# One weight load of a decode kernel, split by partitions into loads of 112, 8 and 8 rows

## The chip, the cores and the metric

The kernel runs on one core of a Trainium2 chip. Its time is device microseconds; the median of three runs before the change is 128.26 us (128.17 to 128.54). The profile is of one further execution of the same program, which took 128.43 us.

## The reference

One token (x, 576 numbers) is normalized and goes through two branches, whose results are added to it.

```python
xn = _layernorm(x)                                   # x: (1, 1, 576)
q  = (xn @ wq)                                       # 32 heads of 128
k, v = the last 4096 of 65536 cached positions       # 16 heads, each used by two query heads
A  = softmax(q k^T * 128**-0.5) v, flattened, @ wo   # wo: (4096, 576)
z  = gelu(xn @ w_in)                                 # w_in: (576, 4608)
B  = (z[:2304] * (w_sp * layernorm(z[2304:]) + b_sp)) @ w_out
out = x + A + B
```

All tensors are bfloat16. The kernel has to read 16.8 MB of keys, 16.8 MB of values and about 17.4 MB of weights, and it writes 576 numbers.

## The kernel before

**Loads.** All large loads are issued from the SP queue, in the order in which they are written at lines 106 to 124: w_q in three pieces, the first block of keys (k0) in two pieces, k1, v0, k2, v1, k3, w_in in two pieces, v2, v3, w_o in three, w_out in five. A block of keys or values holds four heads, 4 MB, 32 KB for each of the 128 partitions. Three tiny loads (the row x_row and two single numbers, ws2) go through the ACT queue at lines 77 to 80.

**The load that is changed.** w_q is read as 1152 half rows of 2048 numbers; partition p holds half rows 9p to 9p+8, which lie one after the other in memory. `load` at line 91 cuts this by half rows:

```python
load(wq_t, wq_v, 2048, (0, 2, 4, NR))      # line 106, NR = 9
```

This makes three loads over all 128 partitions: two of two half rows (8 KB for a partition) and one of five (20 KB for a partition, 2560 KB in all).

**Buffers.** Large tiles share two pools, `small` and `large`, of two buffers each. So k2 can only be issued when the transposes of k0 have ended, v1 when the products of w_q have ended, and so on down the list; SP waits at such a load, and everything after it in the list waits with it. Each load takes the next of eight completion semaphores in turn; a load that takes one again waits until the load that had it last has landed.

**Work on the loads.** `q_ps` (line 223) multiplies the nine half rows by the normalized x, four matmuls for each. `turn(b)` (line 214) transposes a block of keys in eight VectorE instructions; `scores(b)` (line 259) multiplies them by q and prepares the softmax; `values(b)` (line 293) multiplies by the values. The order is written out by hand: turn 0, scores 0, turn 1, scores 1, values 0, and so on to scores 3, then the gated branch (`z_all`, line 317, and `gate`), values 2 and 3, the products with w_o and the first eight rows of w_out (line 391), and last the other ten rows of w_out (line 399), the copy `res` (line 408) and the store of the result (line 409).

## Time and profile before

| What | Value |
|---|---|
| Median of three runs | 128.26 us |
| Profiled execution | 128.43 us, its span 126.6 us |
| Read from memory | 50.96 MB |
| DMA, mean over the span | 403 GB/s |
| PE (matmuls) busy | 76.3 us, 60% |
| DVE (VectorE) busy | 65.6 us, 52% |
| ACT busy | 10.2 us, 8% |
| Mean granted TensorE clock | 0.794 |

The span runs from the first to the last instruction; 1.8 us of the execution's time lie outside of it. Engines in the profile: PE is the matmul, PEld the load of its weights, DVE is VectorE, ACT ScalarE, SP the engine that issues the loads, and SPq its queue. The trace also has a record for every packet that a DMA engine moved (start, duration, bytes, queue) and for every step of a completion semaphore; it does not say which of the 16 DMA engines a record belongs to.

### The profile page before, as it was taken

How to read it: one execution, taken by the hardware profiler on the slowest of the kernel's cores; microseconds unless marked ns; L12 is line 12 of the kernel's file. 1: busy time of each engine (PE TensorE's matmuls, PEld its weight loads, DVE VectorE, ACT ScalarE, POOL GpSimd, SP SyncE). 2: the span in 40 equal slices, each digit the busy share in tenths (PEclk: the TensorE clock that was granted, in tenths of full speed). 3: DMA queues.
4: the chain of work that ended last, by engine and by line, in shares of the span. 5: the costliest groups of instructions: out<-in, count | busy, mean ns of one | idle time of the engine just before them, and what ended most of it. 6: DMA issues, size and time to landing. Idle time of an engine off the chain costs nothing.

```text
span 126.6 us, 1380 instructions
## 1 busy us (share of the span) xinstructions
PE 76.3 (60%) x562; PEld 35.0 (28%) x562; DVE 65.6 (52%) x133; ACT 10.2 (8%) x19; POOL 3.9 (3%) x10
## 2 busy tenths in 40 slices
PE   3241435995179946339963729991960865757470
PEld 3120211331023413313422403330730432423240
DVE  6660069996599844079953169944438400040010
ACT  4010000000300003100003100003000110100010
POOL 8400000000000000000000000000000000000000
PEclk9999999999756999955999975698555595865555
DMA  4999999998998999989999899898999989999930
GB/s 101 427 445 440 430 424 450 430 497 383 448 471 352 476 404 435 476 362 476 404 435 476 382 459 454 384 454 387 487 393 440 455 366 418 433 405 423 400 138 0
DMA packets 3187, 51.03 MB, mean 403 GB/s; under 512 B 365, under 2 KB 622, under 8 KB 1134
## 3 DMA queue, kind: packets, MB, share of 16 engines
q1 hardware_dynamic: 3176, 50.96, 94.8%
q8 instruction: 4, 0.07, 0.2%
q14 instruction: 1, 0.01, 0.0%
q10 hardware_dynamic: 6, 0.00, 0.0%
HBM read 50.96 MB, written 0.00 MB: 402 GB/s over the span
## 4 chain that ended last, share of the span: by engine, by line
DMA 78%; PE 10%; DVE 6%; SPq 2%; ACT 1%; issue 1%; ACTq 0%
DMA k<-in_A_k_cache_dram 37%; DMA v<-in_A_v_cache_dram 27%; DMA wout<-in_B_w_out_dram 14%; PE s L259 8%; DVE kt L214 5%; PE pv L293 1%; ACT p L279 1%; SPq L93 1%; SPq L99 1%; DVE sm L262 1%; PE tr L270 0%; PE su L283 0%; PE fin L399 0%; DVE res L408 0%; DVE m L272 0%
## 5 line engine op out<-in xcount | busy, mean ns | idle before, releaser
L259 PE MATMUL s<-kt,zq 128*128 128x512 bf16 x128 | 38.4, 465 | 10.3 <-DVE kt L214 10.1
L214 DVE STREAM_TRANSPOSE kt<-k 128x1024 f32<-128x1024 f32 x32 | 36.6, 1208 | 3.1 <-DMA k<-in_A_k_cache_dram 3.1
L259 PEld LDWEIGHTS <-zq 128*128 128x128 bf16 x128 | 14.6, 114 | 32.9 <-issue 23.0
L293 PE MATMUL pv<-v,pt 128*32 128x512 bf16 x128 | 10.2, 477 | 1.9 <-DMA v<-in_A_v_cache_dram 1.9
L279 ACT ACTIVATE p<-sm,nm 128x1024 bf16<-128x1024 f32 x4 | 4.6, 1147 | 71.1 <-DVE nm L275 71.1
L304 DVE TENSOR_TENSOR o_t<-op,rm 128x8 bf16<-128x8 f32 x4 | 0.7, 166 | 15.0 <-PE op L301 15.0
L223 PE MATMUL q_ps<-wq,xw 128*32 128x512 bf16 x36 | 4.2, 627 | 6.6 <-DMA wq<-in_A_wq_dram 4.3
L262 DVE CUSTOM_DVE_ANT_1 sm<-s,cm 128x512 f32<-128x512 f32 x8 | 5.4, 672 | 4.7 <-PE s L259 4.7
L281 DVE STREAM_TRANSPOSE pt<-p 128x1024 bf16<-128x1024 bf16 x4 | 5.0, 1245 | 5.4 <-ACT p L279 5.4
L283 PE MATMUL su<-sel,l 128*128 128x8 f32 x8 | 1.8, 293 | 7.6 <-ACT p L279 7.6
L301 PE MATMUL op<-selu,pvs 128*128 128x8 f32 x32 | 4.2, 259 | 2.8 <-ACT pvs L298 2.8
L293 PEld LDWEIGHTS <-pt 128*32 128x32 bf16 x128 | 3.7, 118 | 6.6 <-issue 3.2
L301 PEld LDWEIGHTS op<-selu,pvs 128*128 128x128 f32 x32 | 3.9, 191 | 4.8 <-ACT pvs L298 4.8
L391 PE MATMUL acc<-wo,o_p 128*1 128x288 bf16 x64 | 4.4, 439 | 0.8 <-DMA wo<-in_A_wo_dram 0.8
L395 DVE COPY acc_sb<-acc 128x288 f32<-128x288 f32 x1 | 0.5, 459 | 8.4 <-PE acc L391 8.4
L227 DVE CAST q_sb<-q_ps 128x512 bf16<-128x512 f32 x1 | 0.7, 692 | 7.5 <-PE q_ps L223 7.5
L317 PE MATMUL z<-win,xw 128*32 128x288 bf16 x72 | 4.5, 446 | 0.0
L270 PE MATMUL tr<-ident_f,m 128*128 128x128 f32 x8 | 1.9, 326 | 3.9 <-DVE m L268 3.9
L223 PEld LDWEIGHTS <-xw 128*32 128x32 bf16 x36 | 1.4, 130 | 8.6 <-issue 8.6
L283 PEld LDWEIGHTS su<-sel,l 128*128 128x128 f32 x8 | 1.4, 218 | 8.4 <-ACT p L279 8.4
L298 ACT COPY pvs<-pv 128x512 f32<-128x512 f32 x4 | 2.3, 586 | 13.0 <-PE pv L293 13.0
L346 PE MATMUL sz_ps<-sz,ones_f 128*128 128x2 f32 x2 | 0.6, 362 | 4.6 <-DVE sz L343 4.6
(95 smaller groups left out, 45.1 us busy)
## 6 DMA issues: line engine op xcount, KB each, us to landing
v<-in_A_v_cache_dram SPq DMA_DIRECT2D x4, 4096.0 KB, 32.3
k<-in_A_k_cache_dram SPq DMA_DIRECT2D x3, 4096.0 KB, 30.6
win<-in_B_w_in_dram SPq DMA_DIRECT2D x1, 4608.0 KB, 34.2
k<-in_A_k_cache_dram SPq DMA_DIRECT2D x2, 2048.0 KB, 19.1
wo<-in_A_wo_dram SPq DMA_DIRECT2D x2, 2016.0 KB
wq<-in_A_wq_dram SPq DMA_DIRECT2D x1, 2560.0 KB, 12.6
wq<-in_A_wq_dram SPq DMA_DIRECT2D x2, 1024.0 KB, 6.9
wout<-in_B_w_out_dram SPq DMA_DIRECT2D x1, 1152.0 KB, 25.3
```

What stands on the lines that cost most here:

```text
L214: nc.vector.transpose(t[:].rearrange("p c n e -> p (c n e)").bitcast(FP32), kn[b][:, UK * DH * k:UK * DH * (k + 1)].bitcast(FP32).rearrang ...
L223: nc.tensor.matmul(q_ps[32 * g:32 * g + 32, :], lhsT=xw[:, r, :], rhs=wq_t[:, 2048 * r + 512 * g:2048 * r + 512 * (g + 1)], start=r == 0, ...
L259: nc.tensor.matmul(s_ps[:], lhsT=zq[:, b, ce, ZPAD - 8 * k4:ZPAD - 8 * k4 + P], rhs=kt[b, 4 * kk + k4][:, c, :, e], start=k4 == 0 and ce = ...
L262: nc.vector.tensor_tensor_reduce(out=sm[:, kk, :].rearrange("p (n s) -> p n s", s=HB), in0=s_ps[:].rearrange("p (n s) -> p n s", s=HB), in ...
L279: nc.scalar.activation(p[:], sm[:].rearrange("p k n -> p (k n)"), ACT.Exp, bias=nm[:], accum_out=l[:])
L281: nc.vector.transpose(p_t[b][:].rearrange("p k u m -> p (k u m)"), p[:])
L283: nc.tensor.matmul(su[:], lhsT=l[:].to_broadcast([P, P]), rhs=sel8[:], start=True, stop=True)
L293: nc.tensor.matmul(pv[32 * g:32 * g + 32, :].rearrange("p (n d) -> p n d", n=4), lhsT=p_t[b][:, kk, u, :], rhs=v4[:, kk, u, :, :], start=k ...
L298: nc.scalar.copy(pvs[:], pv[:])
L301: nc.tensor.matmul(op[:], lhsT=pvs[:, DH * u:DH * (u + 1)], rhs=selu[:, 8 * u:8 * u + 8], start=u == 0, stop=u == 3)
L317: nc.tensor.matmul(zp[i][32 * g:32 * g + 32, :], lhsT=xw[:, r, :], rhs=rhs, start=r == 0, stop=r == NR - 1, tile_position=(0, 32 * g))
L391: nc.tensor.matmul(acc[i][32 * g:32 * g + 1, :], lhsT=col, rhs=w[:, HW * i:HW * (i + 1)], start=n == 0 and g > 0, stop=n + 4 >= len(rows), ...
```

## The change

The last piece of w_q, five half rows for each partition, is no longer loaded for all 128 partitions at once, but in three loads: partitions 0 to 111, 112 to 119 and 120 to 127. Each moves the same 20 KB for a partition as before. The bytes, the tile, and all other instructions are the same; SP issues two loads more, at the third place of its list, and each later load takes the completion semaphore two further on in the round of eight.

```diff
     wq_t = unit("wq", LARGE)
-    load(wq_t, wq_v, 2048, (0, 2, 4, NR))
+    load(wq_t, wq_v, 2048, (0, 2, 4))
+    for a, e in ((0, 112), (112, 120), (120, P)):
+        nc.sync.dma_start(wq_t[a:e, 4 * 2048:], wq_v[a:e, 4 * 2048:])
     kn[0] = load_kv(A_k_cache, "k", 0, SMALL, (0, NU // 2, NU))
```

## The prediction

> **What bounds the kernel now.** I read the DMA row of the page first, then the chain of waits, then stretches, then single packets and landings.

> ```profile
> DMA  4999999998998999989999899898999989999930
> GB/s 101 427 445 440 430 424 450 430 497 383 448 471 352 476 404 435 476 362 476 404 435 476 382 459 454 384 454 387 487 393 440 455 366 418 433 405 423 400 138 0
> ```

> Each digit is 3.2 us. The DMA engines are full from the second slice to the last but one. The chain that ended last is 78% DMA, and its end shows what the kernel waits for:

> ```profile
> 71.19 34.61 DMA v<-in_A_v_cache_dram
> 105.80 0.02 issue
> 105.82 17.43 DMA wout<-in_B_w_out_dram
> 123.25 0.04 issue
> 123.29 0.32 PE fin L399 x4
> 123.61 0.02 issue
> 123.63 0.31 DVE res L408
> ```

> The last piece of w_out lands at 123.25, and 3.4 us (four matmuls, a copy, the store) follow to the span's end at 126.6. The stretches say the same with a number: a DMA share of 0.99 to 1.02 everywhere between 2 and 120 us.

> ```profile
> 2.00:14.00 12.00, 3.84 (x28) 2.46 (x29) 5.32 (x21) 1.58 (x3) 2.54 (x3) 1.00 0.99 412
> 14.00:24.00 10.00, 6.30 (x36) 2.48 (x36) 6.65 (x11) 0.00 (x0) 0.00 (x0) 1.00 1.02 439
> 71.00:106.00 35.00, 21.78 (x166) 11.03 (x166) 17.84 (x39) 3.15 (x7) 0.00 (x0) 0.69 0.99 424
> 106.00:120.00 14.00, 9.60 (x115) 4.29 (x111) 1.34 (x6) 0.59 (x1) 0.00 (x0) 0.62 1.00 418
> ```

> The packet records make it sharper. On one engine a packet starts 3 to 4 ns before its predecessor ends, so the records fall into 16 chains, one for each engine, and none has a hole from 1.8 us until its last packet. A 20 KB packet (one row of the changed load) takes 761 ns, 26.9 GB/s; 32 KB takes 1218 ns. At the end, when eleven engines are done, the other five go on at the same 51 ns for 1152 bytes: no engine gets faster when others stop. So the kernel's time is the work of its **slowest engine**, plus 3.4 us.

> Which engine is slowest? The 16 landings of the last load are eleven at 121.30 to 121.78, then 122.41, 122.92, 123.04, 123.17 and 123.25. Five engines are late, and what makes them late is fetched instructions:

> ```profile
> q8 instruction: 4, 0.07, 0.2%
> q14 instruction: 1, 0.01, 0.0%
> ```

> The four packets of q8 (16 KB, at 36.8, 73.2, 96.4 and 119.0 us) and the one of q14 (8 KB, 34.1 us) fall on five chains. Around the one at 36.8, the fetch takes 1099 ns and the next 32 KB packet 1681 instead of 1218: 1.5 us that this engine never makes up. At the landings of the last block of values the four engines hit by then stand 0.65 to 1.5 us behind the rest.

> **The change part by part.** Bytes are the same; what changes is who carries them, and where they go.

> *Rows for each engine.* A load over 128 partitions shows eight packets a chain. Small loads use fewer engines: both single numbers of ws2 lie on one chain, and the store of four rows has four packets and four landing steps. So 112 rows should be seven for each of 16 engines, and each load of eight rows one for each of the same eight, which I call A; B are the others. A then carries 9 rows instead of 8, B 7. At 761 ns a row that is +0.76 for A and -0.76 for B, plus some 10 ns for A's two more completion packets. [...]

> *Where the rows go.* This is the unknown that decides. In all loads of before, each engine has eight partitions to itself; 26.9 GB/s may be what an engine can carry or what the way into its partitions lets through, and the trace cannot tell these apart. In the new small loads eight engines write into eight neighbouring partitions at once. If the engine is the limit, a row takes 0.76 us there too. If eight partitions share one way, eight rows go one after another: 8 x 0.761 = 6.09 us for each small load. Nearest in the trace is that no group of eight partitions is ever filled at more than 26.9 GB/s, which speaks for the dear side; but neighbours may be spread over more ways than one. I take four rows to a way, 3.04 us a load, between the ends and on the dear side. A's share is then 7 + 4 + 4 = 15 row times instead of 8: 7 x 0.761 = +5.33 us.

> [...]

> *SP's list.* Two loads more, 0.43 us each by the third w_q load, move k0's first half from 2.09 to about 3.0. The new round of semaphores makes k0's second half wait for a tiny load (landed 5.36), k1 for the next (6.09) and v0 for the first piece of w_q (5.66). The engines have work queued until 18.6 us at that time, so this costs nothing; without that cover it would be up to 3 us. Every later load still waits for the load eight places ahead of it, which is the same one as before.

> *What waits for w_q.* Its last piece lands at 14.21 now, by the sum near 19.5. The rest of `q_ps`, the first transposes (19.12) and the issue of k2 (28.67) and v1 (29.36) slide by as much, and so do later issues that hang on transposes or products. The queue covers it: k2 would be issued at 34, and the engines have v0 to carry until 42.9; w_in moves from 50.8 to 56, with v1 queued until 62; the last piece of w_out from 105.8 to 111, with work queued until about 119. So no engine runs dry, and the delay of the slowest engine reaches the end once, not twice. PE and DVE are busy 60% and 52% and slide along.

> *The sum.* [...] Then 123.17 + 5.33 = 128.50 instead of 123.25, +5.25 us. The profiled execution would take 128.43 + 5.25 = 133.7; it lies 0.17 over the median, so **133.5 us**.

> **The rivals.**

> *1. The forecast: the eight engines share the way into eight partitions.* Two rows to a way instead of four and no late engine in A: 7 + 2 + 2 = 11 row times, +2.28, from 121.78 to 124.06, a gain of 0.8 at the end: 129.1. Four rows to a way, and B's next load in the way as well as clashes within the 112 rows: two or three row times more, about 135.5. Eight rows to a way would give 23 row times, +11.4 us, near 139.6; I leave that end out, as it has the whole of eight rows meet. Chance 0.55.

> *2. Each engine is its own limit, and late engines lie in A and B.* Then the 123.17 engine ends at 123.17 + 0.77 = 123.94: +0.7, **129.0 us**. For it: no row shows two engines slowing one another. Chance 0.19.

> *3. Each engine is its own limit, and all five late engines lie in B: faster.* B's last lands at 123.25 - 0.76 = 122.49, A's at 121.78 + 0.77 = 122.55, so -0.7: **127.6 us**. The split would be a balance: it gives the rows to engines that have about 1.5 us to spare. [...] It decides where no engine that lands after 122.48 is in A (123.25 - 0.77). Chance 0.18.

> *4. No change.* Engine-limited, and only the engine of 122.41 is in A: 122.41 + 0.77 = 123.18 against 123.25, **128.2 us**. That the split does not move rows at all (112 rows over 16 engines in some other way) comes out here too. Chance 0.08.

> **How the numbers follow.** About 0.3% (0.4 us) is what a measurement of this kernel can tell from no change. Faster is rival 3, 0.18; same is rival 4, 0.08; slower is the forecast and rival 2, 0.74. The range leaves rival 3 out: from 128.0 to 135.6. The forecast's own range is 129.1 to 135.6.

> **What the next profile would show.** Eight chains with nine packets of 20 KB, eight with seven. In the forecast: packets of 20 KB that take about 3 us instead of 0.76, w_q's last landing near 19.5 instead of 14.2, and from there all landings in two groups some 5 us apart. In rivals 2 to 4: all packets at 0.76, the last landing of w_q near 15.0, two groups 1.5 us apart. I would be wrong in the basis if an engine ran dry behind a late issue, or if the last landing moved otherwise than the slowest chain.

## The result and the profile after

The kernel became slower: 138.03 us (median of four runs, 137.28 to 138.26) against 128.23 us, a ratio of 1.0743 with a 95% interval of 1.0725 to 1.076, or +9.8 us. I had forecast +5.25 us, and a range that ended at 135.6.

The profiled execution took 138.26 us with a span of 136.4. The DMA rows of its page, 3.4 us a digit or number:

```profile
DMA  4999997999999999999999999999999999999920
GB/s 132 428 343 276 195 110 149 427 423 504 403 413 425 447 442 452 403 394 461 442 452 403 394 488 415 432 394 428 461 452 427 403 398 426 430 401 428 372 85 0
```

The engines are as busy as before, but from the third to the seventh slice (7 to 24 us) they move 110 to 343 GB/s instead of some 430. The digits do not show this loss, the bytes do: an engine whose packet takes several times as long still counts as busy (in the second stretch of the changed kernel below, a share of 1.03 at 122 GB/s). From 24 us on, both rows are as before. The same in two stretches, the first two lines from the kernel before, the others from the changed one (columns: stretch, length, the busy times of PE, PEld, DVE, ACT and POOL, clock, DMA share, GB/s):

```profile
7.20:15.80 8.60, 3.45 (x32) 1.43 (x36) 1.87 (x9) 0.00 (x0) 0.00 (x0) 1.00 1.02 437
15.80:23.00 7.20, 3.75 (x20) 1.36 (x13) 5.91 (x11) 0.00 (x0) 0.00 (x0) 1.00 1.01 435
```

```profile
7.20:15.80 8.60, 1.90 (x16) 0.67 (x16) 1.86 (x9) 0.00 (x0) 0.00 (x0) 1.00 1.01 267
15.80:23.00 7.20, 0.00 (x0) 0.00 (x0) 0.00 (x0) 0.00 (x0) 0.00 (x0) 1.00 1.03 122
31.00:120.00 89.00, 62.48 (x370) 28.06 (x369) 53.03 (x93) 8.03 (x15) 0.00 (x0) 0.77 1.00 430
```

The chain of waits of the changed kernel begins and ends so:

```profile
2.83 21.31 DMA wq<-in_A_wq_dram
24.14 0.14 issue
24.27 2.35 PE q_ps L225 x19
...
115.57 17.41 DMA wout<-in_B_w_out_dram
133.02 0.32 PE fin L401 x4
133.36 0.31 DVE res L410
```

The last piece of w_q lands at 24.14 instead of 14.21, 9.9 us later; the last piece of w_out at 132.98 (115.57 + 17.41) instead of 123.25, 9.7 us later. The whole loss arises before 24 us, and reaches the end once.

By packets: in the load of 112 rows each engine moves its seven rows of 20 KB in seven rounds, whose medians are 1.00, 1.31, 1.40, 1.27, 1.01, 1.18 and 1.37 us instead of 0.761 each. The 16 packets of the two loads of eight rows take 2.0 to 3.28 us, median 3.22: in the first load seven take 2.0 to 2.6, in the second all take 3.2 to 3.3, and the engine that ends last has 3.25 and 3.22. With the medians of the seven rounds, 8.53 us together, that makes 8.53 + 2 x 3.22 = 15.0 us, where eight rows took 6.1: +8.9. The last of these packets ends 9.2 us later than before; another 0.7 us lies between its end and its landing (1.08 us, before 0.38).

### The profile page after: what moved, and what is told of

It is laid out like the page before. It is cut to its first block, busy times and chain, and to the rows that moved or that the text cites. A ratio compares the mean times of both kernels' runs of the same rounds, so it can differ in the third digit from the quotient of the medians.

```text
span 136.4 us, 1383 instructions
## 1 busy us (share of the span) xinstructions
PE 78.0 (57%) x562; PEld 36.4 (27%) x562; DVE 65.3 (48%) x133; ACT 10.2 (7%) x19; POOL 3.9 (3%) x10
## 4 chain that ended last, share of the span: by engine, by line
DMA 53%; PE 31%; DVE 8%; ACT 3%; SPq 1%; issue 1%; ACTq 0%
DMA v<-in_A_v_cache_dram 24%; PE s L261 21%; DMA wq<-in_A_wq_dram 16%; DMA wout<-in_B_w_out_dram 13%; PE pv L295 4%; ACT p L281 3%; DVE kt L216 3%; PE q_ps L225 2%; DVE sm L264 2%; PE op L303 1%; PE tr L272 1%; DVE pt L283 1%; SPq L108 1%; PE su L285 1%; DVE m L274 1%
## 5 line engine op out<-in xcount | busy, mean ns | idle before, releaser
L261 PE MATMUL s<-kt,zq 128*128 128x512 bf16 x128 | 37.7, 464 | 7.1 <-DVE kt L216 7.1
L295 PE MATMUL pv<-v,pt 128*32 128x512 bf16 x128 | 12.7, 568 | 2.7 <-DMA v<-in_A_v_cache_dram 2.7
L303 PE MATMUL op<-selu,pvs 128*128 128x8 f32 x32 | 5.9, 311 | 2.8 <-ACT pvs L300 2.8
L303 PEld LDWEIGHTS op<-selu,pvs 128*128 128x128 f32 x32 | 5.5, 259 | 6.0 <-ACT pvs L300 6.0
L393 PE MATMUL acc<-wo,o_p 128*1 128x288 bf16 x64 | 3.7, 387 | 0.4 <-DMA wo<-in_A_wo_dram 0.4
L319 PE MATMUL z<-win,xw 128*32 128x288 bf16 x72 | 3.7, 381 | 0.0
```

What stands on the lines that cost most here:

```text
L261: nc.tensor.matmul(s_ps[:], lhsT=zq[:, b, ce, ZPAD - 8 * k4:ZPAD - 8 * k4 + P], rhs=kt[b, 4 * kk + k4][:, c, :, e], start=k4 == 0 and ce = ...
L295: nc.tensor.matmul(pv[32 * g:32 * g + 32, :].rearrange("p (n d) -> p n d", n=4), lhsT=p_t[b][:, kk, u, :], rhs=v4[:, kk, u, :, :], start=k ...
L303: nc.tensor.matmul(op[:], lhsT=pvs[:, DH * u:DH * (u + 1)], rhs=selu[:, 8 * u:8 * u + 8], start=u == 0, stop=u == 3)
L319: nc.tensor.matmul(zp[i][32 * g:32 * g + 32, :], lhsT=xw[:, r, :], rhs=rhs, start=r == 0, stop=r == NR - 1, tile_position=(0, 32 * g))
L393: nc.tensor.matmul(acc[i][32 * g:32 * g + 1, :], lhsT=col, rhs=w[:, HW * i:HW * (i + 1)], start=n == 0 and g > 0, stop=n + 4 >= len(rows), ...
```

## Experiments

Each diff shows the lines that stand at the place of `load(wq_t, wq_v, 2048, (0, 2, 4, NR))`; all else is the kernel before. Theory P: several engines that write into neighbouring partitions at once share a way of about one engine's rate (26.9 GB/s: 20 KB in 0.761 us before). Its rivals: S, the loads more in SP's list; E, nine rows against seven; R, the reading; later N, odd row counts. Row times are medians of 20 KB packets, with one row of before at 0.761 us.

**The same cut by columns (e1).**

```diff
+    load(wq_t, wq_v, 2048, (0, 2, 4))
+    for a, e in ((0, 8960), (8960, 9600), (9600, 10240)):
+        nc.sync.dma_start(wq_t[:, 8192 + a:8192 + e], wq_v[:, 8192 + a:8192 + e])
```

> The last piece of w_q is cut into three loads as in the change, in the same proportion (7/8, 1/16, 1/16), but by columns: each load still fills all 128 partitions. Theory P (the partitions that are written at once decide: neighbours share a way of about 26.9 GB/s): nothing is lost, 128.2 us, 20 KB rows now in pieces of 17.9, 1.3 and 1.3 KB at the full rate. Theory S (the two loads more in SP's list, and the later round of semaphores, cost the time): 138 us, as the change. Theory E (each engine is its own limit, the loss is that eight engines carry nine rows): 128.2 us.

128.53 us against 128.32, ratio 1.0014 (1.0005 to 1.0023). Two loads more in SP's list, and the shifted round of semaphores, cost about 0.2 us. S falls.

**112 rows and 16 (e2).**

```diff
+    load(wq_t, wq_v, 2048, (0, 2, 4))
+    for a, e in ((0, 112), (112, P)):
+        nc.sync.dma_start(wq_t[a:e, 4 * 2048:], wq_v[a:e, 4 * 2048:])
```

> The last piece of w_q in two loads, partitions 0 to 111 and 112 to 127. Each engine carries seven rows and one, eight as before. Theory P: the 112 rows again take about 8.7 us instead of 5.3 (as in the change's trace), and the 16 rows go to four groups of four neighbours, so that each takes 3.1 to 3.3 us instead of 0.76; w_q lands near 20, 5.9 us later than before, and the kernel takes about 134 us. Theory E (nine rows against seven): 128.2 us, as no engine has more rows than another. Theory S: about 133 us, half of the change's loss, as one load more is issued, but with all packets at 0.76 us.

133.89 us, ratio 1.0446 (1.0419 to 1.0472). Every engine carries eight rows, as before the change, and still 5.6 us are lost: E does not explain these. The seven rounds of the 112 rows take 0.89 to 1.32 us again. The stretch of the load, then the one behind it:

```profile
7.20:15.80 8.60, 1.90 (x16) 0.60 (x16) 1.87 (x9) 0.00 (x0) 0.00 (x0) 1.00 1.15 295
15.80:23.00 7.20, 2.32 (x20) 0.71 (x21) 1.09 (x2) 0.00 (x0) 0.00 (x0) 1.00 0.85 288
```

The 16 rows behind it took 2.1 us (1.26 to 2.50), under the 3.1 to 3.3 that I expected. The engines come to them up to a microsecond apart, and part of the delay shows only in the 16 KB packets right behind them: the first 16 of k0 take 1.0 to 2.2 us instead of 0.61.

**The destination alone (e3, e4).** Four loads of eight rows of 4 KB into a tile that nothing reads. The two kernels differ only in the partitions written:

```diff
     load(wq_t, wq_v, 2048, (0, 2, 4, NR))
+    extra = ktp.tile([P, 2048], BF16, name="extra", tag="kt")
+    for a in (96, 104, 112, 120):                                               # e3
+        nc.sync.dma_start(extra[a:a + 8, :], wq_v[112:120, 8192:10240])         # e3
+    for a in (0, 1, 32, 33):                                                    # e4
+        nc.sync.dma_start(extra[a:a + 29:4, :], wq_v[112:120, 8192:10240])      # e4
```

> The three loads of w_q as before, and behind them four further loads of eight rows of 4 KB into a tile that nothing reads, at partitions 96 to 103, 104 to 111, 112 to 119 and 120 to 127 (the same eight rows of w_q as source each time). Eight engines carry 16 KB more each. Theory P with four rows to a way: a row takes about 0.61 us instead of 0.15, so the four loads hold the eight engines up by 2.4 us; 130.6 us if one of the latest engines is among them, about 129.2 us if not. Theory E: 0.6 us, 128.8 us at most. Theory P with eight to a way: 1.22 us a row, 4.9 us, 133 us.

> As e3_near, the same four loads with the same source rows, the same eight engines and the same bytes, but into partitions four apart: 0, 4, to 28; 1, 5, to 29; 32, 36, to 60; 33, 37, to 61. Theory P: no two engines write neighbours, so a row takes 0.15 us, four loads 0.6 us: 128.8 us if one of the latest engines is among the eight, 128.2 us if not; at least 1 us under e3_near. Theory E and a theory R (it is the reading of few rows by few engines that is slow, wherever they go): the same time as e3_near. The small packets also mark the eight engines, and so show in which half the late ones lie.

Neighbours 129.94 us (1.0121, 1.0105 to 1.0136), four apart 128.98 (1.0047, 1.0032 to 1.0062). The stretch in which these packets run, first e3, then e4:

```profile
13.20:15.20 2.00, 0.25 (x4) 0.13 (x7) 0.00 (x0) 0.00 (x0) 0.00 (x0) 1.00 1.07 254
```

```profile
13.20:15.20 2.00, 1.02 (x12) 0.49 (x15) 0.00 (x0) 0.00 (x0) 0.00 (x0) 1.00 1.01 426
```

The same bytes, sources and engines: 254 GB/s into neighbours, 426 into partitions four apart. In e4 all 32 packets take 159 ns. In e3 half of them do, and the rest up to 456. Most of the delay shows in the 16 KB packets that run beside and behind them, which take up to 1.35 us instead of 0.61, some of them begun after the last 4 KB packet had ended. The cost was 1.6 us, not the 2.4 that four to a way would give. R falls for the loads of eight rows. Further, e4's small packets mark the eight engines: of the instruction fetches, the one at 31.0 us and, as far as the chains can be followed that late, the one at 94.6 fall on marked chains, and the one at 37.7 on another. (The one at 74.5 cannot be given to a group: its chain is one of a marked and an unmarked one that coincide from 18.97 us on.) So late engines lie in both groups, and +0.66 us for 4 x 159 ns = 0.64 us says that one of the latest is among the marked.

**Halves, and even and odd (e5, e6).**

```diff
+    load(wq_t, wq_v, 2048, (0, 2, 4))
+    for a, e in ((0, 64), (64, P)):                                             # e5
+        nc.sync.dma_start(wq_t[a:e, 4 * 2048:], wq_v[a:e, 4 * 2048:])           # e5
+    for a in (0, 1):                                                            # e6
+        nc.sync.dma_start(wq_t[a:P:2, 4 * 2048:], wq_v[a:P:2, 4 * 2048:])       # e6
```

> The last piece of w_q in two loads of 64 rows, the even partitions and the odd ones. Each load reaches all groups of four neighbours. Theory P8, rows dealt out in order: an engine's four rows are 8e, 8e+2, 8e+4 and 8e+6, so engines four apart fill the same way at the same time, 1.52 us a row and 134.4 us, though all 16 ways are within the load's reach; if the engines fall out of step, less, down to 128.3 us. Theory P4 and theory R: 128.3 us.

Halves 134.94 us (1.0513, 1.0496 to 1.0531), even and odd 128.33 us (0.9999, 0.999 to 1.0008). First e5, then e6:

```profile
7.20:15.80 8.60, 1.90 (x16) 0.61 (x16) 1.86 (x9) 0.00 (x0) 0.00 (x0) 1.00 1.06 231
```

```profile
7.20:15.80 8.60, 3.58 (x32) 1.21 (x36) 1.87 (x9) 0.00 (x0) 0.00 (x0) 1.00 1.00 430
```

64 neighbours run at about half the rate: 1.61 us a row instead of 0.761. The same 64 rows a load, every second partition, run at 0.761 us from the first row on. P4 falls (e5) and P8 stands. My dealing of the rows in plain order was wrong for e6: by P8 no two engines can have met on a way there.

**The small loads alone (e7).** The change with every second partition in its loads of eight:

```diff
+    load(wq_t, wq_v, 2048, (0, 2, 4))
+    nc.sync.dma_start(wq_t[0:112, 4 * 2048:], wq_v[0:112, 4 * 2048:])
+    for a in (112, 113):
+        nc.sync.dma_start(wq_t[a:P:2, 4 * 2048:], wq_v[a:P:2, 4 * 2048:])
```

> The change with its first load untouched (partitions 0 to 111) and the two loads of eight rows dealt otherwise: 112, 114, to 126, and 113, 115, to 127. The same bytes, engines and sources in number; two neighbours of a group of four are written at once instead of four. Theory P: a row of these loads takes 1.5 to 1.7 us instead of 3.2, w_q lands 3.2 us earlier than in the change, near 21, and the kernel takes about 134.8 us. Theory R and theory E: 138 us as the change.

135.33 us, ratio 1.0544 (1.0519 to 1.057): 2.7 us of the change's loss come back by dealing the same 16 rows otherwise. Their packets take 1.97 us (median) instead of 3.22; I had expected 1.5 to 1.7.

**Fewer bytes (e8).** The split on a piece of 8 KB rows:

```diff
+    load(wq_t, wq_v, 2048, (0, 2))
+    for a, e in ((0, 112), (112, 120), (120, P)):
+        nc.sync.dma_start(wq_t[a:e, 2 * 2048:4 * 2048], wq_v[a:e, 2 * 2048:4 * 2048])
+    nc.sync.dma_start(wq_t[:, 4 * 2048:], wq_v[:, 4 * 2048:])
```

> The split into 112, 8 and 8 is made on the second piece of w_q (two half rows, 8 KB for a partition) instead of the last one (20 KB), which is one load again. Theory P: a loss of bandwidth, in proportion to the bytes, 2/5 of the change's 9.8 us: 132.2 us, rows of 8 KB at 1.3 us in the loads of eight (0.31 before) and about 0.5 us in the load of 112. Theory S or any fixed cost of such a load: 138 us.

131.44 us, ratio 1.0241 (1.0223 to 1.026): +3.1 us, not the fixed 9.8, and somewhat under 2/5 of it. The 112 rows run at 0.31 to 0.49 us a row (0.309 before), the loads of eight at 0.65 (up to 1.11), half of what I expected there. As in e3, the packets of the short rows show only a part: the 20 KB packets behind them have a first round of 1.95 us (median) instead of 0.761, and summed over the engines that is more than the short rows themselves lost.

**What makes 112 rows slow (e9 to e12).** Still open was whether odd row counts are slow as such.

```diff
+    load(wq_t, wq_v, 2048, (0, 2, 4))
+    for a in range(8):                                                          # e9; e10: range(7)
+        nc.sync.dma_start(wq_t[a:P:8, 4 * 2048:], wq_v[a:P:8, 4 * 2048:])       # e9, e10
+    for a in (7, 71):                                                           # e10
+        nc.sync.dma_start(wq_t[a:a + 57:8, 4 * 2048:], wq_v[a:a + 57:8, 4 * 2048:])
+    for a in range(4):                                                          # e11
+        nc.sync.dma_start(wq_t[a:P:4, 4 * 2048:], wq_v[a:P:4, 4 * 2048:])       # e11
+    for a in range(7):                                                          # e12
+        nc.sync.dma_start(wq_t[a:a + 106:7, 4 * 2048:], wq_v[a:a + 106:7, 4 * 2048:])
+    nc.sync.dma_start(wq_t[112:P, 4 * 2048:], wq_v[112:P, 4 * 2048:])           # e12
```

> The last piece of w_q in eight loads of 16 rows, partitions a, a+8, to a+120 for a = 0 to 7: one row for each engine and load. Open is why the change's load of 112 rows takes 8.7 us, 1.2 to 1.4 us a row. Theory P (it is which partitions are written at the same moment): each load spreads over all 16 blocks of eight partitions; if the engines are matched to ways as in e6_even_odd, 0.76 us a row and 128.4 us; if they are dealt in plain order, two to a way, 1.6 us a row and 134.9 us as e5_halves. Theory N (a load of other than 128 or 64 rows is slow whatever it writes, or many loads are): over 1.2 us a row, 132 us or more. Theory S (each load in SP's list costs about 4 us): far over 140 us.

> The change's shares without its neighbours: seven loads of 16 rows as in e9 (a = 0 to 6, 112 rows, seven for each engine), then partitions 7, 15, to 63 and 71, 79, to 127 in two loads of eight rows. The same eight engines carry nine rows, the others seven. Theory P: the seven loads run as in e9, 5.3 us for 112 rows if that is 0.76 us a row; the loads of eight reach four ways each, two engines to a way, about 1.6 us a row, so the eight engines end 0.76 + 2 x 0.85 = 2.5 us later and the kernel takes about 130.8 us. Theory E (each engine its own limit): 129.0 us. If the nine rows against seven were a gain that collisions hid: below 128 us.

> The last piece of w_q in four loads of 32 rows, partitions a, a+4, to a+124 for a = 0 to 3: two rows for each engine and load, one row in each group of four neighbours. Open after e9: whether every load of other than 128 or 64 rows is slow (theory N), or only one in which two engines write to the same way at a time (theory P8). Theory N: over 1.2 us a row, 132 us or more. Theory P8 with plain order of dealing (as e9 fits): engine e writes groups 2e and 2e+1, engines four apart share a way, 1.6 us a row, 134.8 us. Theory P8 with the dealing of e6_even_odd, each engine its own way: 0.76 us a row, 128.4 us; this alone excludes N.

> The 112 rows of e2_112_16 in seven loads of 16 rows, partitions a, a+7, to a+105 for a = 0 to 6, then partitions 112 to 127 in one load as in e2. If a load of 112 rows is dealt in plain order, engine e has rows 7e to 7e+6, and these seven loads give each engine the same rows in the same order. Theory P8: then the row times repeat those of the 112-row load round by round (about 1.0, 1.3, 1.4, 1.25, 1.0, 1.2, 1.3 us, between one and two engines to a way), 133.9 us as e2. If the 112 rows are dealt otherwise: another pattern, 0.76 to 1.6 us a row and 131 to 136 us.

| Run | us | Ratio (95%) | Row time |
|---|---|---|---|
| e9, 8 loads of 16, step 8 | 134.80 | 1.0507 (1.0483 to 1.0531) | 1.35 in the first round, then 1.45 to 1.58 |
| e10, 7 of 16, step 8, and 2 of 8 | 136.71 | 1.0644 (1.0623 to 1.0665) | 1.31 to 1.60; the last 1.61 |
| e11, 4 loads of 32, step 4 | 128.47 | 0.9999 (0.999 to 1.0008) | 0.761, every packet |
| e12, 7 of 16, step 7, and 16 | 133.89 | 1.0462 (1.0403 to 1.052) | 0.84, 1.32, 1.28, 1.31, 0.86, 1.14, 1.28 |

The same stretch of e9 and of e11:

```profile
7.20:15.80 8.60, 2.08 (x16) 0.52 (x16) 1.86 (x9) 0.00 (x0) 0.00 (x0) 1.00 1.05 223
```

```profile
7.20:15.80 8.60, 3.42 (x32) 1.39 (x36) 1.87 (x9) 0.00 (x0) 0.00 (x0) 1.00 1.01 434
```

e11 excludes N: its loads of 32 rows, each with one row in every group of four, run at the full rate, 0.761 us a row. e9 is P8 whatever the dealing, and against P4: by P8, 16 partitions eight apart lie on eight ways, two to each, which is 2 x 0.761 = 1.52 us a row, and 1.45 to 1.58 were measured behind the first round. So my 0.76 us for "matched" engines was not to be had, and e9 says nothing on the dealing. e10's expected 130.8 stood on 0.76 us for its seven loads; with e9's row time it had to be near e9, and its two loads of eight add 1.9 us. e12 gives each engine the rows that plain dealing gives it in a load of 112, and lands on e2's time and nearly its pattern (0.89, 1.30, 1.32, 1.19, 1.05, 1.20, 1.28).

## Why the prediction was wrong

**The basis held.** The end moves with the work of the slowest engine: 9.9 us at w_q, 9.7 us at the last landing, 9.8 us in the median. No chain of packets has a hole after 25 us, so the late issues of k2 (38.34 us instead of my 34) and what follows were covered. SP's list cost next to nothing (0.2 us in e1), as said.

**The mechanism was right, its price for the small loads nearly so.** e3 and e4 differ in nothing but the partitions written, and their stretch ran at 254 and at 426 GB/s. I took 3.04 us a row for eight neighbours, between 0.76 and 6.09; measured were 3.22 (median; less in the first load, see above). That it was four rows to a way I had not read from a trace; it was a choice between two ends. 8 x 20 KB in 3.22 us are 51 GB/s for eight neighbours, about two engines' rate (2 x 26.9). In e5, 16 x 20 KB in 1.61 us are 204 GB/s for 64 neighbours, under half of the 430 in e6's stretch. P8 is the layout that fits the runs best: groups of four fit the 4.2 row times of the small loads (3.22/0.761) and, less closely, the 1.97 us of e7, which writes two of each four at once; beside e4, whose partitions four apart ran at 426 GB/s, e5 and e9 (1.61 and 1.45 to 1.58 us a row) need ways that partitions further apart share. P8 puts these 32 apart; no run tried one such pair alone. And a load need not span all 128 partitions for the full rate here: e6 and e11 run at it (430 and 434 GB/s) with loads of 64 and 32 partitions that are spread over the whole.

**The start of the sum.** That the engine which lands at 123.17 is in A, and takes on all of the +5.33, is not shown, for the kernel before or for the changed one. What e4 showed in its place: the chain fetched for at 94.6 is among the eight marked ones, and 0.64 us of packets on these eight cost the kernel 0.66 us.

**The step that failed is the first term of 7 + 4 + 4.** I charged the load of 112 rows 7 x 0.761 = 5.33 us, as if only its share changed, and asked of the small loads alone where their rows go. It took 8.53. This is 3.2 us of the 4.6 by which the forecast fell short (9.8 - 5.25); e2, which has that load and no uneven shares, loses 5.6 us. Seven rows do not divide into groups of four, so with plain dealing an engine's run straddles groups, and by P8 engines meet on a way. What such meetings cost is read from e5 and e9 (1.61 and 1.45 to 1.58 us a row) against e6 and e11 (0.761), and e12 (133.89 us, as e2) shows that the 112 rows lose their time by which partitions are written together. Why engines that by P8 are alone on their way are slow as well stays open (last section). Of the rest, 2 x (3.22 - 3.04) = 0.4 us is the row time; the remaining 0.9 us I have not traced to a term.

**The range** named clashes within the 112 rows as "two or three row times more, about 135.5" and counted B's hindrance into the same; the clashes alone were worth 4.2 row times.

**The two groups of landings some 5 us apart did not come.** The first half of k0 lands in two groups of eight, 26.66 to 27.30 and 28.16 to 28.78, some 1.5 us apart: the two rows' difference at 0.76 us that rivals 2 to 4 had. I had taken it that B runs free while A waits. The trace shows all 16 engines held up: while the small loads run, the 16 KB packets of k0, to which B has gone on, take 1.1 to 2.9 us (the first 32 of them, median 2.4) instead of 0.61. 16 KB in 2.4 us are 6.8 GB/s, 20 KB in 3.22 us are 6.4: in this time B gained next to nothing on A.

**Rivals 2 to 4** needed packets of 0.76 us, which did not occur. Their question got an answer too: late engines lie in both groups in e4. If they do so in the changed kernel too, which is not shown, rival 3 was not to be had, and without shared ways the outcome would have been rival 2, slower.

## What to carry to other kernels

Here a split by partitions changed which partitions are written at the same moment, and this cost more than the shares it moved: 9.8 us, where one row more for eight engines is 0.76 us of work. Before such a split, count for each load, all rows of the largest one included, how many engines write into the same four neighbours at a time (3.22 us a row for eight neighbours instead of 0.761), and into partitions that P8 puts on one way, 32 apart (1.45 to 1.58 us in e9). Of the splits of this load, those into runs of neighbours cost 5.6 to 9.8 us (e2, e5, the change), those by columns (e1, 128.53 us) and into every second or every fourth of the 128 partitions (e6, 128.33, e11, 128.47) 0.2 us or less: try the latter first. The full DMA row of the change did not mean a full rate (a share of 1.03 at 122 GB/s): read the GB/s under it, then packet durations.

## What the runs showed that I had not expected

Engines that by P8 have a way to themselves were slow too. With the ways as in theory P8 and plain dealing, the 112 rows leave 12 of 16 engines alone on their way in most rounds, yet in the second round no packet is under 1.27 us; and B's packets above stretch fourfold (2.4 us instead of 0.61), all eight engines', though by P8 the partitions 112 to 127 make up only four ways. The last packet of the second small load takes 3.22 us, although the other seven end 1.1 to 2.0 us before it. Where this blocking sits was not tried and stays open, and so does which rows an engine gets in loads of 32, 64 and 128, beyond that e6 and e11 fit an engine with its own way.

The packets of short rows look better than their loads are. In the loads of eight neighbours a row took 3.22/0.761 = 4.2 times as long at 20 KB, 0.65/0.309 = 2.1 times at 8 KB, and half of the 4 KB packets of e3 no longer than in e4, but much of the delay then shows in the packets behind them. In the kernel's time the gap is smaller: e8 lost 3.1 us where a loss in proportion to the bytes would be 3.9, e3 cost 1.6 where I expected 2.4. What is left of it may be short rows, or engines that did not all meet; this was not tried.
